# Shared scattering of two small expert groups, k maxima a slice ahead, and another order of the attention front

## The chip, the cores and the metric

The kernel runs on one core of a Trainium2 chip. A core has the matrix engine (TensorE, "PE" in the profile), the vector engine (VectorE, "DVE"), the scalar engine (ScalarE, "ACT"), GpSimd ("POOL") and SyncE ("SP", which here issues the loads and stores). Each engine works through its own queue of instructions in order and waits on semaphores for the others. The metric is the device time of one execution in microseconds (us).

## The reference

The computation has three stages. First comes an attention without a score matrix: the softmax of q runs over the head's 64 features, that of k over the 576 positions, and each head multiplies q by the 64x64 product of k and v. Its output is x, 2304 tokens of 512 features. Then two mixture-of-experts layers follow, each token going to the expert with the highest logit.

```
q_s = exp(q - max(q, over d));  q_s /= sum(q_s, over d) + 1e-9      # [4, 8, 576, 64]
k_s = exp(k - max(k, over s));  k_s /= sum(k_s, over s) + 1e-9
x   = einsum(q_s, einsum(k_s, v))                                   # as 2304 x 512

# layer 1: expert = argmax(x @ w_gate); at most 576 tokens of one expert are kept
out[i] = gate_w[i] * (relu(x[i] @ w1[e]) @ w2[e])      # 512 -> 1024 -> 512, 8 experts

# layer 2, with its own weights, only for tokens with x @ w_skip > 0
out[i] = x[i] + gate_w[i] * (relu(x[i] @ w1[e]) @ w2[e])
```

## The kernel before

**Data.** x is kept transposed, one tile X[b] for each batch b: 128 feature rows, 4 chunks of features, 576 tokens. A batch's 8 heads are two halves of 4 heads, named a and b (batch 0), c and d (1), e and f (2), g and i (3). A half goes through the attention in small steps, the methods of `Half`: `qm` (maxima of q, negated, in `mx`), `q1` to `q3` or `exp_sub` with `exp_act` (exp), `qn` or `inverse` with `norm` (division by the sums `qz`), `qt` or `turn` (transposes of q), `km` (column maxima of k, three operations on DVE that leave `m`), `kt` (transposes of m, tile `pt`, L386), `kc` (subtraction), `ke` (exp), `kv` (products k·v, into `kd`, shown as `kvd`), `re` (products q·kv, tile `px`, copied into x by ACT).

**Dense groups.** Nearly all tokens of a batch go to one expert, so for the five pairs of layer and batch in the table `COURSE`, (0,0), (0,1), (0,2), (1,0) and (1,1), the kernel runs that expert over all 576 tokens of the batch, with a gate (`gm`, `pg`, `mg`) that is zero elsewhere. Each of these groups has 16 slices, 8 for w1 and 8 for w2. A float32 operand is split into a high and a low part (`split`: ACT casts the high part `wh` or `xh`, DVE subtracts, giving `wl` or `xl`), and each product is three matmuls of 128 x 288 (`products`, `first_products`; lines L822, L842, L863). A slice runs in this order: `products(i)`, `split_w(i+2)`, the words of its line in `COURSE` to the left of the bar, `evacuate(i)` (ACT's relu `hh`, L876, and DVE's remainder `hl`, L877, or the gated sums), and then the words to the right of the bar. So the table sets the order of instructions on every engine. A word like `d.km` is a method of a half, `G.0` one of the gate's, `L4` a load of weights, `S.u00` a step of a small group.

**Small groups.** The few tokens of other experts, at most 32 for an expert, go through `Small`: S is the group of (0,2) with one expert, T that of (1,2) with two experts. Words `t` are the steps of an expert (`expert(t, step)`; the last one leaves its output in `y2`, a high and a low part: four quarters of partitions), `v` and `a` make the one-hot matrix pT of the tokens' places (`places`, `place`), and `u` scatters, `put`: for two chunks of features and two halves of tokens, two matmuls `pts` (L1255, 128 x 288 each, over all 128 partitions) and an addition to x on DVE (L1259). `y2` is zero outside of what an expert has written. `S.u00 S.u01` stand in the last slice of (0,2); `T.u00`, `T.u01` in slices 3 and 4 of (1,1), and `T.u10`, `T.u11` in its slices 10 and 11.

**Front.** Ahead of `COURSE` stands the attention of batch 0 (code from L950 to L1112), written out in one order for all engines: `k_v` is the product of k and v of a half (L992), `k_v_norm` divides it, `q_norm` divides q, `q_turn` and `q_last` transpose q (L463, L470), `x_main` and `x_last` multiply by kv (L495, L489). `H01` and `H23` are the two pairs of heads in a half: exps of H01 come from a subtraction (`exp_sub`) and one large exp (`exp_act`, L344), those of H23 from small exps with the sums included (`exps`, L334). `guess` (L568 to L587) finds, from kv alone, which expert batch 0 will use, and leaves its number in `gid`; SP reads gid and then issues the first loads of weights (`ws`). `warm_up(n)` (L535) issues n dummy matmuls on PE. At the front's end `first_products` (48 matmuls, L822) does slices 0 and 1 of the first group. The lines of the front around the change are:

```
        k_v(a)
        warm_up(16)
        v_ones(b)
...
        a.exp_sub(H01, ALLJ)
...
        k_v(b)
...
        a.sum_bulk(H01, ALLJ)
        RT["C0"].guess()
...
        q_norm(a, H01)
        q_norm(a, H23)
        warm_up(8)
```

Of the kernel before, what the change touches and what calls it, by code (L numbers as in the profile page):

```python
# [95 lines left out]
    N3 | S.t04  # L96
    X3 | S.u00 S.u01
    """),
    ((1, 0), """
    L4 G.3 | g.rw  # L100
    g.rx | M2.1
# [18 lines left out]
    L5 i.rx | T.t04 C3.1  # L120
    T.v1 | T.t10 T.u00
    L6 | T.u01 C3.2 G.1
    C3.3 | T.t11 C3.4 O0.3
# [3 lines left out]
    | T.t14  # L127
    | T.u10
    | T.u11 O1.0
    | O2.0  # L130
# [8 lines left out]
def kernel(  # L139
# [810 lines left out]
    with tc.tile_pool(name="fp", bufs=1) as fp:  # L950
# [57 lines left out]

        def q_norm(h, hs):
            h.inverse(hs)  # L1010
            h.norm(hs)

# [35 lines left out]
        k_v(a)  # L1048
        warm_up(16)
        v_ones(b)  # L1050
        k_exp(b)
        a.qm()
        a.exp_sub(H01, ALLJ)
        a.exps([(2, j) for j in range(NJ)])
        a.exp_act(H01, ALLJ)
        k_v(b)
        k_v_norm(a)
        b.qm()
        a.exps([(3, j) for j in range(NJ)])
        warm_up(12)  # L1060
        b.exp_sub(H01, ALLJ)
# [4 lines left out]
        a.sum_bulk(H01, ALLJ)  # L1066
        RT["C0"].guess()
# [10 lines left out]
        H["d"].load_v()  # L1078
        q_norm(a, H01)
        q_norm(a, H23)  # L1080
        warm_up(8)
        a.turn_new()
        q_turn(a, 0)
        warm_up(3)
        q_turn(a, 1)
# [4 lines left out]
        x_main(a, 0)  # L1090
        warm_up(2)
        x_main(a, 1)
        x_last(a)
        first.split_x(0)
        first.split_x(1)
        first.split_w(0)
        warm_up(2)
        b.turn_new()
        q_turn(b, 0)
        warm_up(3)  # L1100
        q_turn(b, 1)
        q_last(b)
        first.first_products(0, range(0, 2))
        first.split_w(1)
        x_main(b, 0)
        x_main(b, 1)
        x_last(b)
        first.first_products(1, range(0, 2))
        first.split_x(2)
        first.split_x(3)  # L1110
        first.first_products(0, range(2, 4))
        first.first_products(1, range(2, 4))  # L1112
# [9 lines left out]
    class Small:  # L1122
# [69 lines left out]
        def expert(self, t, step):  # L1192
# [4 lines left out]
            if step != 2:  # L1197
                for i in {0: (0, 1), 1: (2, 3), 3: (4, 5), 4: (6, 7)}[step]:
                    w = self.tw.pop(8 * t + i)
                    for g in range(4):  # L1200
                        if i < 4:
# [4 lines left out]
                        nc.tensor.matmul(  # L1206
                            out=self.ph[32 * g:32 * g + 32, :256], lhsT=lhsT, rhs=rhs, start=(i % 4 == 0), stop=(i % 4 == 3)
                        )
                    self.load(8 * t + i + 3)
# [9 lines left out]
            elif step == 4:  # L1219
                for i in range(2):  # L1220
                    sl, cs = slice(64 * i, 64 * i + 64), slice(2 * i, 2 * i + 2)
                    src = self.ph[sl, :256].rearrange("p (c d) -> p c d", c=2)
                    nc.scalar.copy(y2[0][sl, cs], src)
                    nc.vector.tensor_sub(y2[1][sl, cs], src, y2[0][sl, cs].bitcast(F32))

        def places(self, t):
            cs = hp.tile([P, TINY], F32, name="cs2", tag="cs2")
            nc.vector.tensor_scalar(out=cs, in0=iota, scalar1=self.r["tlo"][:, t:t + 1], scalar2=None, op0=ALU.add)
            self.p4 = hp.tile([P, NJ, 4, TINY], F32, name="p4", tag="ot", bufs=3)
            bb = [P, NJ, TINY]  # L1230
            for g in range(4):
                nc.vector.tensor_tensor(
                    out=self.p4[:, :, g],
                    in0=self.r["z"].unsqueeze(2).to_broadcast(bb),
                    in1=cs.unsqueeze(1).to_broadcast(bb),
                    op=ALU.is_equal,
                )
# [11 lines left out]

        def put(self, t, i):  # L1250
            for c in (2 * i, 2 * i + 1):
                for a in range(2):
                    pt = bank("pts")
                    for n, u in enumerate(y2):
                        nc.tensor.matmul(  # L1255
                            out=pt[:, :HT], lhsT=u[:, c], rhs=self.pT[t][:, tokens(a)], start=(n == 0), stop=(n == 1)
                        )
# [223 lines left out]
```

## Time and profile before

| quantity | value |
|---|---|
| three runs, median (lowest to highest) | 416.97 us (416.24 to 419.02) |
| the profiled execution | 416.55 us |
| its span, first to last instruction | 414.7 us |
| PE busy in it | 393.7 us |
| fillers L535 | 94 matmuls, 18.7 us |
| scattering L1255 | 48 matmuls |

All times of the sections below are those of the profiled execution, in us from the start of its span. Busy times of matmuls overlap in PE's pipeline, so a sum of them can exceed the span; the distance from one matmul's start to the next one's start tells what it costs. In a row of a timeline the columns are start, duration, engine, line, operation, written tile, read tiles, sizes and count, and in brackets the idle time ahead of it with the instruction that ended it.

### The profile page before, as it was taken

How to read it: one execution, taken by the hardware profiler on the slowest of the kernel's cores; microseconds unless marked ns; L12 is line 12 of the kernel's file. 1: busy time of each engine (PE TensorE's matmuls, PEld its weight loads, DVE VectorE, ACT ScalarE, POOL GpSimd, SP SyncE). 2: the span in 40 equal slices, each digit the busy share in tenths (PEclk: the TensorE clock that was granted, in tenths of full speed). 3: DMA queues.
4: the chain of work that ended last, by engine and by line, in shares of the span. 5: the costliest groups of instructions: out<-in, count | busy, mean ns of one | idle time of the engine just before them, and what ended most of it. 6: DMA issues, size and time to landing. Idle time of an engine off the chain costs nothing.

```text
span 414.7 us, 8456 instructions
## 1 busy us (share of the span) xinstructions
PE 393.7 (95%) x3241; PEld 351.1 (85%) x3241; DVE 251.6 (61%) x640; ACT 182.3 (44%) x547; POOL 12.4 (3%) x46
## 2 busy tenths in 40 slices
PE   8989898999999999999999999999999999899892
PEld 4656797898999989799999888899998988799881
DVE  4874789463586846278546656367777736654432
ACT  1656675734357772324346622333375342331211
POOL 2400000000000000000000100000000000000000
PEclk9999999999999999999999999999999999999998
DMA  8829926100970400293355771116315556363133
GB/s 207 220 54 262 255 72 193 31 2 2 295 182 9 124 2 2 82 300 96 107 195 178 217 216 52 51 52 232 101 53 183 182 180 214 92 204 123 31 101 102
DMA packets 72535, 54.48 MB, mean 131 GB/s; under 512 B 18454, under 2 KB 67114, under 8 KB 72490
## 3 DMA queue, kind: packets, MB, share of 16 engines
q1 hardware_dynamic: 70536, 53.60, 44.4%
q10 hardware_dynamic: 1954, 0.31, 0.6%
q8 instruction: 26, 0.43, 0.4%
q14 instruction: 19, 0.16, 0.1%
HBM read 49.16 MB, written 4.73 MB: 130 GB/s over the span
## 4 chain that ended last, share of the span: by engine, by line
PE 85%; DVE 8%; ACT 3%; issue 2%; DVEq 0%; ACTq 0%
PE pair L863 31%; PE pair L842 25%; PE pair L535 3%; PE px L495 3%; PE pxs L1150 2%; PE pk L437 2%; PE pl L596 2%; PE pto L1284 2%; PE ph L1206 1%; PE py L1206 1%; PE pts L1255 1%; PE pk L992 1%; PE ptq L463 1%; DVE hl L877 1%; PE pair L822 1%
## 5 line engine op out<-in xcount | busy, mean ns | idle before, releaser
L863 PE MATMUL pair<-hh,wh 128*128 128x288 f32 x320 | 98.3, 307 | 0.0
L863 PE MATMUL pair<-hh,wl 128*128 128x288 f32 x320 | 94.6, 296 | 0.0
L863 PE MATMUL pair<-hl,wh 128*128 128x288 f32 x320 | 94.5, 295 | 0.0
L842 PE MATMUL pair<-xh,wh 128*128 128x288 f32 x304 | 92.8, 305 | 0.0
L842 PE MATMUL pair<-xl,wh 128*128 128x288 f32 x304 | 89.6, 295 | 0.0
L842 PE MATMUL pair<-xh,wl 128*128 128x288 f32 x304 | 89.5, 295 | 0.0
L785 DVE TENSOR_TENSOR wl<-ws,wh 128x512 fp32r<-128x512 f32 x80 | 54.9, 686 | 35.9 <-ACT wh L784 35.4
L863 PEld LDWEIGHTS pair<-hh,wh 128*128 128x128 f32 x320 | 60.5, 189 | 3.8 <-issue 2.6
L863 PEld LDWEIGHTS pair<-hl,wh 128*128 128x128 f32 x320 | 60.7, 190 | 0.1
L876 ACT ACTIVATE hh<-pair 128x576 fp32r<-128x576 f32 x40 | 25.8, 645 | 79.2 <-PE pair L842 77.4
L863 PEld LDWEIGHTS pair<-hh,wl 128*128 128x128 f32 x320 | 60.5, 189 | 0.0
L842 PEld LDWEIGHTS pair<-xh,wh 128*128 128x128 f32 x304 | 57.1, 188 | 2.2 <-issue 0.9
L842 PEld LDWEIGHTS pair<-xl,wh 128*128 128x128 f32 x304 | 57.2, 188 | 0.1
L842 PEld LDWEIGHTS pair<-xh,wl 128*128 128x128 f32 x304 | 57.1, 188 | 0.0
L877 DVE SCALAR_TENSOR_TENSOR hl<-pair,hh 128x576 fp32r<-128x576 f32 x40 | 30.2, 755 | 37.1 <-ACT hh L876 37.1
L784 ACT CAST wh<-ws 128x512 fp32r<-128x512 f32 x80 | 49.3, 620 | 2.2 <-DMA ws<-in_moe_w_dram 1.5
L334 ACT ACTIVATE eq<-qt,mx 128x64 f32<-128x64 f32 x140 | 46.7, 338 | 0.5 <-DVE mx L323 0.5
L334 ACT ACTIVATION_READ_ACCUMULATOR eq<-qt,mx 128x1 f32 x140 | 26.6, 190 | 0.0
L535 PE MATMUL pair<-warm 128*128 128x384 f16 x94 | 18.7, 346 | 1.6 <-DVE warm L952 1.6
L785 DVE TENSOR_TENSOR xl<-x,xh 128x576 fp32r<-128x576 f32 x20 | 14.9, 752 | 6.0 <-ACT xh L784 6.0
L1285 ACT COPY ot<-pto 128x256 f32<-128x256 f32 (+1 forms) x24 | 7.0, 315 | 26.0 <-PE pto L1284 26.0
L535 PEld LDWEIGHTS <-warm 128*128 128x128 f16 x94 | 9.3, 104 | 8.1 <-issue 2.1
(210 smaller groups left out, 500.2 us busy)
## 6 DMA issues: line engine op xcount, KB each, us to landing
ws<-in_moe_w_dram SPq DMA_DIRECT2D x39, 512.0 KB, 4.7
tw<-in_moe_w_dram SPq DMA_DIRECT2D x24, 512.0 KB, 4.6
kt<-in_k_dram SPq DMA_DIRECT2D x8, 512.0 KB, 7.5
qt<-in_q_dram SPq DMA_DIRECT2D x8, 512.0 KB, 6.5
out_dram<-ot SPq DMA_DIRECT2D x12, 256.0 KB, 2.7
vt<-in_v_dram SPq DMA_DIRECT2D x16, 128.0 KB, 4.8
vt<-in_v_dram SPq DMA_DIRECT2D x3, 512.0 KB
mg<-gate SPq DMA_DIRECT2D x4, 288.0 KB, 7.2
```

Of the source, the lines that this page charges most:

```text
L334: nc.scalar.activation(self.eqv[:, h, j], self.qt[:, h, j], AF.Exp, bias=self.mx[:, i:i + 1], accum_out=self.qz[:, i:i + 1])
L437: nc.tensor.matmul(out=pk[64 * g:64 * g + 64, c * D1 + o:c * D1 + o + n], lhsT=self.kt[:rows(j), 2 * c + g, j], rhs=ones32[:rows(j), 0:1] ...
L495: nc.tensor.matmul(out=pt, lhsT=self.kd[:, c], rhs=self.qT[:, c, 0:4 * P], start=True, stop=True)
L535: nc.tensor.matmul(out=pw[:, 0, :3 * P], lhsT=warm16[:, 0:P], rhs=warm16, start=True, stop=True)
L596: nc.tensor.matmul(out=pl[32 * c:32 * c + 32, :HT], lhsT=self.weights[:, c], rhs=self.chunk(c, tokens(a)), start=True, stop=True,)
L784: nc.scalar.copy(hi, src)
L785: nc.vector.tensor_tensor(out=lo, in0=src, in1=hi.bitcast(F32), op=ALU.subtract)
L842: nc.tensor.matmul(out=self.pt[:, a, :HT], lhsT=u[:, c], rhs=w[:, c, tokens(a)], start=(c == 0 and n == 0), stop=(c == NC - 1 and n == 2),)
L863: nc.tensor.matmul(out=self.pt[:, a, :HT], lhsT=p_[:, f], rhs=w[:, tokens(a)], start=(v == 0 and f == 0 and n == 0), stop=(v == 1 and f == ...
L876: nc.scalar.activation(halves(hh), src, AF.Relu)
L877: nc.vector.scalar_tensor_tensor(out=halves(hl), in0=src, scalar=0.0, in1=halves(hh).bitcast(F32), op0=ALU.max, op1=ALU.subtract,)
L1150: nc.tensor.matmul(out=self.px[:, c * self.w:(c + 1) * self.w], lhsT=self.xt[:rows(j), c * P:(c + 1) * P], rhs=self.pj[:rows(j), j], start ...
```

## The change

Three things change. Names are as above.

1. **Scattering.** `put(t, i)` becomes `put(i)`. The second expert of T (t = 1) writes its outputs to the mirrored halves of the partitions of `y2`, and `places` builds one-hots of both experts into each pT, so that one set of matmuls scatters both. `T.u00` and `T.u01` are gone; `T.u10`, `T.u11` become `T.u0`, `T.u1` in the same slices. `S.u00 S.u01` become `S.u0` in the same slice and `S.u1` behind the evacuation of the first slice of (1,0).
2. **Maxima of k.** `d.km`, `e.km` and `f.km` move from the left side of a slice's bar to the right side of the bar one slice earlier.
3. **Front.** The subtraction for H01 goes from DVE to GpSimd (`q_sub`). `k_v(b)` stands behind 4 instead of 16 fillers, the sums and the first `q_norm` of a stand ahead of `guess`. The turns and products of b stand between those of a and ahead of all dense products, which now follow one another. Fillers are 74 instead of 94.

The diff, with one of the three moved maxima and the code of the front and of the scattering (the lines of dots are places left out):

```
-    C0.5 c.qn d.q1 |
-    L7 d.km | c.qt d.kt
+    C0.5 c.qn d.q1 | d.km
+    L7 | c.qt d.kt
...
-    X3 | S.u00 S.u01
+    X3 | S.u0
     """),
     ((1, 0), """
-    L4 G.3 | g.rw
+    L4 G.3 | S.u1 g.rw
     g.rx | M2.1
...
-    T.v1 | T.t10 T.u00
-    L6 | T.u01 C3.2 G.1
+    T.v1 | T.t10
+    L6 | C3.2 G.1
...
-    | T.u10
-    | T.u11 O1.0
+    | T.u0
+    | T.u1 O1.0
...
-        def q_norm(h, hs):
+        def q_norm(h, hs, eng=None):
             h.inverse(hs)
-            h.norm(hs)
+            (eng or nc.vector).tensor_tensor(
+                out=h.eqv[:, hs], in0=h.eqv[:, hs], in1=h.spread_q(h.qz, hs, ALLJ), op=ALU.mult
+            )
+
+        def q_sub(h):
+            nc.gpsimd.tensor_tensor(
+                out=h.eqv[:, H01], in0=h.qt[:, H01], in1=h.spread_q(h.mx, H01, ALLJ), op=ALU.add
+            )
 
         def q_turn(h, c):
             pt = bank("ptq")
...
         warm_up(2)
         k_sub(b)
         k_v(a)
-        warm_up(16)
         v_ones(b)
         k_exp(b)
         a.qm()
-        a.exp_sub(H01, ALLJ)
+        q_sub(a)
+        warm_up(4)
+        k_v(b)
         a.exps([(2, j) for j in range(NJ)])
         a.exp_act(H01, ALLJ)
-        k_v(b)
         k_v_norm(a)
         b.qm()
+        q_sub(b)
         a.exps([(3, j) for j in range(NJ)])
-        warm_up(12)
-        b.exp_sub(H01, ALLJ)
+        a.sum_bulk(H01, ALLJ)
+        warm_up(6)
         k_v_norm(b)
         b.exps([(2, j) for j in range(NJ)])
         b.exp_act(H01, ALLJ)
         b.exps([(3, j) for j in range(NJ)])
-        a.sum_bulk(H01, ALLJ)
+        q_norm(a, H01)
         RT["C0"].guess()
         first.eid = load_reg(gid[0], [ET.SP], 7)
         first.load(0, 0)
...
         H["d"].load_q()
         H["d"].load_k()
         H["d"].load_v()
-        q_norm(a, H01)
-        q_norm(a, H23)
-        warm_up(8)
+        warm_up(2)
         a.turn_new()
         q_turn(a, 0)
-        warm_up(3)
+        q_norm(a, H23)
+        warm_up(4)
         q_turn(a, 1)
         q_last(a)
         b.sum_bulk(H01, ALLJ)
...
         q_norm(b, H23)
         x_main(a, 0)
         warm_up(2)
+        b.turn_new()
+        q_turn(b, 0)
         x_main(a, 1)
         x_last(a)
-        first.split_x(0)
-        first.split_x(1)
-        first.split_w(0)
         warm_up(2)
-        b.turn_new()
-        q_turn(b, 0)
-        warm_up(3)
         q_turn(b, 1)
         q_last(b)
-        first.first_products(0, range(0, 2))
-        first.split_w(1)
+        first.split_x(0)
         x_main(b, 0)
+        first.split_x(1)
+        warm_up(2)
         x_main(b, 1)
         x_last(b)
-        first.first_products(1, range(0, 2))
+        first.split_w(0)
+        warm_up(4)
+        first.first_products(0, range(0, 2))
         first.split_x(2)
         first.split_x(3)
+        first.split_w(1)
+        first.first_products(1, range(0, 2))
         first.first_products(0, range(2, 4))
         first.first_products(1, range(2, 4))
...
                     w = self.tw.pop(8 * t + i)
                     for g in range(4):
+
+                        o = 32 * (g ^ 2 if t and i >= 4 else g)
                         if i < 4:
                             lhsT, rhs = self.xs[:, i, 32 * t:32 * t + 32], w[:, 256 * g:256 * g + 256]
                         else:
                             lhsT = self.hT[:, g % 2, 32 * (i - 4):32 * (i - 4) + 32]
                             rhs = w.rearrange("p (u d) -> p u d", u=2)[:, g % 2, 256 * (g // 2):256 * (g // 2) + 256]
                         nc.tensor.matmul(
-                            out=self.ph[32 * g:32 * g + 32, :256], lhsT=lhsT, rhs=rhs, start=(i % 4 == 0), stop=(i % 4 == 3)
+                            out=self.ph[o:o + 32, :256], lhsT=lhsT, rhs=rhs, start=(i % 4 == 0), stop=(i % 4 == 3)
                         )
                     self.load(8 * t + i + 3)
             if step == 1:
...
                 nc.vector.tensor_copy(out=self.hT, in_=pt[:, :2 * P].rearrange("p (u s) -> p u s", u=2))
             elif step == 4:
                 for i in range(2):
-                    sl, cs = slice(64 * i, 64 * i + 64), slice(2 * i, 2 * i + 2)
+                    o = 64 * (i ^ t)
+                    sl, cs = slice(o, o + 64), slice(2 * i, 2 * i + 2)
                     src = self.ph[sl, :256].rearrange("p (c d) -> p c d", c=2)
                     nc.scalar.copy(y2[0][sl, cs], src)
                     nc.vector.tensor_sub(y2[1][sl, cs], src, y2[0][sl, cs].bitcast(F32))
 
         def places(self, t):
-            cs = hp.tile([P, TINY], F32, name="cs2", tag="cs2")
-            nc.vector.tensor_scalar(out=cs, in0=iota, scalar1=self.r["tlo"][:, t:t + 1], scalar2=None, op0=ALU.add)
+            cs = hp.tile([P, 2, TINY], F32, name="cs2", tag="cs2")
+            for u in range(self.n):
+                nc.vector.tensor_scalar(
+                    out=cs[:, u], in0=iota, scalar1=self.r["tlo"][:, u:u + 1], scalar2=None, op0=ALU.add
+                )
             self.p4 = hp.tile([P, NJ, 4, TINY], F32, name="p4", tag="ot", bufs=3)
             bb = [P, NJ, TINY]
             for g in range(4):
                 nc.vector.tensor_tensor(
                     out=self.p4[:, :, g],
                     in0=self.r["z"].unsqueeze(2).to_broadcast(bb),
-                    in1=cs.unsqueeze(1).to_broadcast(bb),
+                    in1=cs[:, (g // 2) ^ t if self.n == 2 else 0].unsqueeze(1).to_broadcast(bb),
                     op=ALU.is_equal,
                 )
 
...
             nc.tensor.transpose(pt[:, 0:LAST], p4f[:LAST, 4], ident[:LAST, :LAST])
             nc.scalar.copy(pT[:, 4 * P:S], pt[:, 0:LAST])
 
-        def put(self, t, i):
+        def put(self, i):
+            pT = self.pT[i if self.n == 2 else 0]
             for c in (2 * i, 2 * i + 1):
                 for a in range(2):
                     pt = bank("pts")
                     for n, u in enumerate(y2):
                         nc.tensor.matmul(
-                            out=pt[:, :HT], lhsT=u[:, c], rhs=self.pT[t][:, tokens(a)], start=(n == 0), stop=(n == 1)
+                            out=pt[:, :HT], lhsT=u[:, c], rhs=pT[:, tokens(a)], start=(n == 0), stop=(n == 1)
                         )
                     x = self.x[:, c, tokens(a)]
                     nc.vector.tensor_add(x, x, pt[:, :HT])
```

The order of instructions at three places where it moves. First GpSimd's queue in the front, as a difference of the two programs; `va` and `vt` hold v of half b, `eq` and `qt` the exps and q of a (and then b), `mx` the negated maxima.

```order
 L985 COPY va<-vt 128x4x64 x4
 L985 COPY va<-vt 64x4x64
+L1016 ISA
+L1016 TENSOR_TENSOR eq<-qt,mx 128x2x5x64 x2
 L297 MEMSET kt 64x4x64
 L302 MEMSET vt 128x20
```

Two subtractions have come in behind the copies of v and ahead of the fills for later halves, with one instruction of another kind ahead of them.

Next DVE's queue in the front, from the subtraction of b to the guess, as a difference; L1003 to L1007 are `k_v_norm`, L320 and L323 `qm`, L348 the sums, L362 to L367 (L1011 in the change) `q_norm`, L572 the start of the guess.

```order
-L339 TENSOR_TENSOR eq<-qt,mx 128x2x5x64
+L348 TENSOR_REDUCE qz<-eq 128x10
 L1003 TENSOR_SCALAR rz<-pk 128x2
 L1004 RECIPROCAL rz<-rz 128x2
 L1007 TENSOR_TENSOR kvd_115<-pk,rz 64x2x64 x2
-L348 TENSOR_REDUCE qz<-eq 128x10
+L362 TENSOR_SCALAR qz<-qz 128x10
+L363 RECIPROCAL qz<-qz 128x10
+L1011 TENSOR_TENSOR eq<-eq,qz 128x2x5x64
 L572 COPY gx<-pgx 128x4
```

The subtraction is gone (that of a is gone ahead of it in the same way), the sums of a have moved ahead of the norm of kv(b), and the first norm of a's q stands ahead of the guess instead of behind it.

Last DVE's queue in the second half of the first dense group, where the maxima of d are made (L378 to L380, tile m) between the remainders `hl` of two slices; of before:

```order
L877 SCALAR_TENSOR_TENSOR hl<-pair_83,hh 128x576
L785 TENSOR_TENSOR wl_206<-ws_198,wh_202 128x512
L378 TENSOR_TENSOR m_959<-kt 128x512
L379 TENSOR_TENSOR m_960<-m_959 128x256
L380 TENSOR_TENSOR m_960<-m_960,kt 128x256
L877 SCALAR_TENSOR_TENSOR hl<-pair_84,hh 128x576
```

and of the change:

```order
L877 SCALAR_TENSOR_TENSOR hl<-pair_84,hh 128x576
L378 TENSOR_TENSOR m_912<-kt 128x512
L379 TENSOR_TENSOR m_913<-m_912 128x256
L380 TENSOR_TENSOR m_913<-m_913,kt 128x256
L785 TENSOR_TENSOR wl_206<-ws_198,wh_202 128x512
L877 SCALAR_TENSOR_TENSOR hl<-pair_83,hh 128x576
```

The three operations for m now stand ahead of the split `wl`, which stands behind them.

## Rows read from the trace of the kernel before

**Rows 1.** Page, part 1: busy us, share of the span, instructions of each engine.

```profile
PE 393.7 (95%) x3241; PEld 351.1 (85%) x3241; DVE 251.6 (61%) x640; ACT 182.3 (44%) x547; POOL 12.4 (3%) x46
```

**Rows 2.** PE's waits: line, waited for; us in total, times, longest.

```profile
PE pt L386 <- DVE m L380: 3.4, 4, 1.6
```

**Rows 3.** PE's timeline of the front: start, us, engine, line, operation, count.

```profile
16.75 2.77 PE L535 MATMUL pair<-warm 128*128 128x384 f16 x16
19.36 2.98 PE L992 MATMUL pk<-va,kt 128*128 128x130 f32 x20
...
29.28 0.63 PE L463 MATMUL ptq<-c,eq 128*128 128x128 f32 x4
...
36.01 0.40 PE L822 MATMUL pair<-xh,wl 128*128 128x288 f32 x1 [0.44 <-DVE wl L785]
...
37.44 1.88 PE L495 MATMUL px<-qT,kvd 128*128 128x512 f32 x4
...
39.52 0.38 PE L822 MATMUL pair<-xh,wh 128*128 128x288 f32 x1
...
45.17 1.18 PE L596 MATMUL pl<-x,wg 128*32 128x288 f32 x16
```

**Rows 4.** DVE's timeline of the front.

```profile
17.02 0.83 DVE L339 TENSOR_TENSOR eq<-qt,mx 128x640 f32<-128x640 f32 x1
...
22.38 0.16 DVE L1003 TENSOR_SCALAR rz<-pk 128x2 f32<-128x2 f32 x1 [1.05 <-PE pk L992]
...
23.40 0.82 DVE L348 TENSOR_REDUCE qz<-eq 128x10 f32<-128x640 f32 x1
25.22 0.16 DVE L572 COPY gx<-pgx 128x4 f32<-128x4 f32 x1 [1.01 <-PE pgx L568]
...
26.62 0.14 DVE L587 TENSOR_SCALAR gid<-gid 1x1 int32<-1x1 int32 x1
...
27.86 0.17 DVE L362 TENSOR_SCALAR qz<-qz 128x10 f32<-128x10 f32 x1
...
29.05 0.81 DVE L348 TENSOR_REDUCE qz<-eq 128x10 f32<-128x640 f32 x1
```

**Rows 5.** Timelines of POOL and of ACT in the front.

```profile
15.19 1.76 POOL L985 COPY va<-vt 128x256 f32<-128x256 f32 x5 [2.29 <-DMA vt<-in_v_dram]
...
1.80 1.28 ACT L221 ACT_TABLE_LOAD   x1 [1.80 <-issue]
...
18.69 0.72 ACT L344 ACTIVATE eq<-eq 128x640 f32<-128x640 f32 x1
```

**Rows 6.** Page, part 6: DMA issues, count, KB each, median us to landing.

```profile
ws<-in_moe_w_dram SPq DMA_DIRECT2D x39, 512.0 KB, 4.7
...
kt<-in_k_dram SPq DMA_DIRECT2D x8, 512.0 KB, 7.5
```

**Rows 7.** Timelines of DVE and PE around the maxima of d.

```profile
68.72 0.68 DVE L785 TENSOR_TENSOR wl<-ws,wh 128x512 fp32r<-128x512 f32 x1
...
71.13 0.41 PE L386 MATMUL pt<-c,m 128*128 128x128 f32 x2 [1.64 <-DVE m L380]
...
80.37 1.52 PE L936 MATMUL pg<-c,gm 128*128 128x128 f32 x10
```

**Rows 8.** Windows, line L1255 alone: S.u00 with S.u01, T.u00, T.u01; length, PE.

```profile
253.38:256.63 3.25, 2.83 (x16) 2.21 (x16) 1.00 0.58 166
347.92:349.38 1.46, 1.44 (x8) 1.13 (x8) 1.00 0.56 101
352.55:354.97 2.42, 1.32 (x8) 1.02 (x8) 1.00 0.57 165
```

**Rows 9.** Windows: length, PE, PEld, DVE, ACT, POOL, granted clock, DMA, GB/s.

```profile
1.55:4.55 3.00, 3.00 (x10) 1.48 (x11) 0.00 (x0) 1.49 (x2) 1.83 (x9) 1.00 0.80 215
4.55:7.23 2.68, 2.68 (x19) 1.58 (x17) 1.54 (x3) 0.00 (x0) 0.00 (x0) 1.00 1.19 273
410.70:414.70 4.00, 0.00 (x0) 0.00 (x0) 0.00 (x0) 0.00 (x0) 0.00 (x0) 0.50 0.17 45
```

More of the change, by code (lines that the diff above doesn't have):

```diff
@@ L1007, in k_v_norm, with q_norm, q_sub @@
                 nc.vector.tensor_mul(h.kd[sl, :, sl], pv[sl, :, g, 0:D], rz[sl].to_broadcast([64, 2, D]))
-        def q_norm(h, hs):
+        def q_norm(h, hs, eng=None):
             h.inverse(hs)
-            h.norm(hs)
+            (eng or nc.vector).tensor_tensor(
+                out=h.eqv[:, hs], in0=h.eqv[:, hs], in1=h.spread_q(h.qz, hs, ALLJ), op=ALU.mult
+            )
+        def q_sub(h):
+            nc.gpsimd.tensor_tensor(
+                out=h.eqv[:, H01], in0=h.qt[:, H01], in1=h.spread_q(h.mx, H01, ALLJ), op=ALU.add
+            )
         def q_turn(h, c):
@@ L1048 @@
         k_v(a)
-        warm_up(16)
         v_ones(b)
@@ L1052 @@
         a.qm()
-        a.exp_sub(H01, ALLJ)
+        q_sub(a)
+        warm_up(4)
+        k_v(b)
         a.exps([(2, j) for j in range(NJ)])
         a.exp_act(H01, ALLJ)
-        k_v(b)
         k_v_norm(a)
         b.qm()
+        q_sub(b)
         a.exps([(3, j) for j in range(NJ)])
-        warm_up(12)
-        b.exp_sub(H01, ALLJ)
+        a.sum_bulk(H01, ALLJ)
+        warm_up(6)
         k_v_norm(b)
@@ L1078 @@
         H["d"].load_v()
-        q_norm(a, H01)
-        q_norm(a, H23)
-        warm_up(8)
+        warm_up(2)
         a.turn_new()
         q_turn(a, 0)
-        warm_up(3)
+        q_norm(a, H23)
+        warm_up(4)
         q_turn(a, 1)
@@ L1091 @@
         warm_up(2)
+        b.turn_new()
+        q_turn(b, 0)
         x_main(a, 1)
         x_last(a)
-        first.split_x(0)
-        first.split_x(1)
-        first.split_w(0)
         warm_up(2)
-        b.turn_new()
-        q_turn(b, 0)
-        warm_up(3)
         q_turn(b, 1)
         q_last(b)
-        first.first_products(0, range(0, 2))
-        first.split_w(1)
+        first.split_x(0)
         x_main(b, 0)
+        first.split_x(1)
+        warm_up(2)
         x_main(b, 1)
         x_last(b)
-        first.first_products(1, range(0, 2))
+        first.split_w(0)
+        warm_up(4)
+        first.first_products(0, range(0, 2))
         first.split_x(2)
         first.split_x(3)
+        first.split_w(1)
+        first.first_products(1, range(0, 2))
         first.first_products(0, range(2, 4))
@@ L1200, in expert @@
                     for g in range(4):
+                        o = 32 * (g ^ 2 if t and i >= 4 else g)
                         if i < 4:
@@ L1206, in expert @@
                         nc.tensor.matmul(
-                            out=self.ph[32 * g:32 * g + 32, :256], lhsT=lhsT, rhs=rhs, start=(i % 4 == 0), stop=(i % 4 == 3)
+                            out=self.ph[o:o + 32, :256], lhsT=lhsT, rhs=rhs, start=(i % 4 == 0), stop=(i % 4 == 3)
                         )
@@ L1226, in places @@
         def places(self, t):
-            cs = hp.tile([P, TINY], F32, name="cs2", tag="cs2")
-            nc.vector.tensor_scalar(out=cs, in0=iota, scalar1=self.r["tlo"][:, t:t + 1], scalar2=None, op0=ALU.add)
+            cs = hp.tile([P, 2, TINY], F32, name="cs2", tag="cs2")
+            for u in range(self.n):
+                nc.vector.tensor_scalar(
+                    out=cs[:, u], in0=iota, scalar1=self.r["tlo"][:, u:u + 1], scalar2=None, op0=ALU.add
+                )
             self.p4 = hp.tile([P, NJ, 4, TINY], F32, name="p4", tag="ot", bufs=3)
@@ L1255, in put @@
                         nc.tensor.matmul(
-                            out=pt[:, :HT], lhsT=u[:, c], rhs=self.pT[t][:, tokens(a)], start=(n == 0), stop=(n == 1)
+                            out=pt[:, :HT], lhsT=u[:, c], rhs=pT[:, tokens(a)], start=(n == 0), stop=(n == 1)
                         )
```

34 lines of the change are left out of this document (18 added, 16 removed).

## The prediction

> **What bounds the kernel now.** I read four views. First, busy time by engine: TensorE (PE) works 393.7 of 414.7 us, DVE 251.6, ACT 182.3, POOL 12.4 [rows 1]. Time is won where PE has less to do or stands less. Second, what PE waited for [rows 2]: its largest entry is four waits, together 3.4 us, of the transposes `pt` for the column maxima `m` of k, which DVE makes. That view hides the front, because fillers (the dummy products of `warm_up`, L535) count as busy. So the third view is PE's timeline of the front, read for what the fillers cover [rows 3]. k_v(a) is done when sixteen fillers start at 16.75; k_v(b) starts only behind them, at 19.36. The second turn of half a starts at 29.28, the long run of dense products (`first_products`, L822) at 36.01, and it ends at 45.17, where the router's logits start; between 37.44 and 39.52 the x of half b cuts it. Fourth, DVE's timeline tells who sets this pace [rows 4]. At 22.38 it has waited 1.05 us for k_v(b); then come the norm of kv(b), a's sums (23.40) and the guess (its copy at 25.22, gid ready at 26.62 + 0.14 = 26.76). Only behind the guess stand the two norms of a's q, the second from 27.86 to 29.05, and the turn at 29.28 needs the second. So the front's chain is k_v(b), DVE's norm, sums, guess and norms, the turns and x of both halves, dense products. Behind 45.17 PE is nearly dense, so what the front saves reaches the end unless a later wait takes it up.
>
> **The front.** Four edits act on this chain.
>
> (1) k_v(b) stands behind 4 fillers instead of 16. Sixteen take 19.36 − 16.75 = 2.61, 0.163 each [rows 3]; k_v(b) starts at 16.75 + 4 × 0.163 = 17.40, 1.96 earlier, and so ends at about 20.4 instead of 22.38.
>
> (2) DVE no longer makes the differences q − max of a and b (0.83 each, the first at 17.02) [rows 4]; POOL does. From 17.02 to 22.38 − 1.05 = 21.33 DVE made both of these, the norm of kv(a) and b's maxima; without the two that is 4.31 − 1.66 = 2.65, so until 19.7. Then a's sums, 0.82, to 20.5; the norm of kv(b), 23.40 − 22.38 = 1.0, to 21.5; a's first q norm, taken like the second's 29.05 − 27.86 = 1.2, to 22.7; from the guess's copy to gid 26.76 − 25.22 = 1.54, to 24.2 (2.5 earlier; the first loads of `ws` wait for gid, and come earlier by as much); the second q norm to 25.4. The second turn of a starts then, 3.8 ahead of 29.28.
>
> (3) From there PE runs the turns and x of a and b's turns as before, 36.01 − 29.28 = 6.73, and now x of b too, 39.52 − 37.44 = 2.08: dense products start at 25.4 + 6.7 + 2.1 = 34.2. Fewer fillers could shorten it, but b's norms follow a's on DVE at the same distance, so I keep the 6.73.
>
> (4) All 48 dense products then run in one piece. Without a wait one takes (37.44 − 36.01) / 10 = 0.143, so 48 take 6.9; with the waits of before, (45.17 − 36.01 − 2.08) / 46 = 0.154, so 7.4. With 7.2 they end at 41.4 against 45.17: **−3.7**; ends −4.0 and −3.5. What could be late is their operands, the splits of x and w by ACT and DVE; one more wait as at 36.01 (0.44) is about the upper end.
>
> The price of the move is POOL's. In before POOL only copies and fills: five copies of 256 elements take 1.76, 0.35 each, until 16.95 [rows 5]. By that, 640 elements are 0.9 if only their count matters; twice that, 1.8, if two inputs are read in turn. Starting at 17.0 this is ready at 17.9 or 18.8. ACT is busy with other exps until it takes this half at 18.69 [rows 5]: hidden in both cases, with 0.8 of cover left or none. The fills queued behind it on POOL are for tiles read only in the dense groups. But the order shows one more instruction there, L1016 ISA, which the built program calls a library reload; before has none. It costs nothing if there is nothing to load. The nearest row is ACT's load of a table, 1.28 [rows 5]; if code has to be fetched by a transfer, the transfers here need 4.7 to 7.5 from issue to landing [rows 6]. I take 1.28, because it is a load that an engine does for itself, like this one; the transfer is rival B. Of 1.28, the cover of 0 to 0.8 hides a part, and 0.3 more is hidden since DVE takes a's sums at 19.7 and ACT's exp (0.72) would be done at 19.4: 0.2 to 1.0 late, **+0.7**, ends 0 and +1.3. Beyond its cover every us on POOL is a us on the chain, for a's sums, the norm of kv(b), the guess and the second norm stand behind it on DVE in that order.
>
> The Trainium skill speaks against this edit: "GPSIMD Engine Reference", §2.1 Instruction dispatch, says that the first call to a freshly loaded kernel pays a code load of about 6 us with no instruction in the profile. No row of before shows such a load. By it this term would be an estimated +5.3 and the sum −1.8.
>
> **The maxima of k.** For d, e and f, DVE makes them ahead of one split `wl` (0.68 at 68.72) instead of behind it [rows 7], so each of three waits can shrink by up to 0.7; d's is 1.64 [rows 7], the others share 3.4 − 1.64, 0.6 each [rows 2]. The split itself comes later by m's three operations, but its products are a slice away. Does PE keep the gain? For d I think not: the gate's ten matmuls start at 80.37 [rows 7], behind ACT's copies of c's x, and ACT's place there follows from work on DVE and ACT that isn't less. For e there is a like join in `gate1`, behind DVE's gm. Only f's is kept: **−0.6**; ends −1.9 and 0.
>
> **The shared scattering.** For T, 16 of 32 matmuls L1255 go, and 8 adds on DVE. The two pieces removed from the middle of group (1,1) took 1.46 and 2.42 [rows 8]; less about 0.2 of pipeline change at their borders: **−3.7**, ends −3.9 and −3.4. The matmuls that stay are as wide as before, and those in the tail are as many as before; half as many do because each partition half now holds one expert's part. One more small operation of `places` on DVE lies beside PE's products. For S no matmul goes; sixteen in one piece took 3.25 [rows 8]. Now its second half stands behind the first evacuation of the next group, as T's second piece did: 1.46 + 2.42 = 3.88, up to 0.3 more for waits on the adds, so **+0.9**, ends +0.6 and +1.2.
>
> **Sum.** −3.7 + 0.7 − 0.6 − 3.7 + 0.9 = −6.4. The profiled execution took 416.55 (span 414.7 and 1.85 around it); the median of the three runs, 416.97, is 0.42 above it. From halfway between, 416.8, I take **410.4**. All low ends together are 2.8 less, all high ends 2.0 more; they don't fall together, so the sum's own range is 408.8 to 412.4. A measurement of this kernel can tell about 1%, 4.2 us, from no change.
>
> **Rivals.** A is the sum above: chance 0.66.
>
> B: the reload is a transfer of code and holds POOL for 6.1 us, the middle of 4.7 and 7.5 [rows 6]. Less 0.3 and the cover of 0 to 0.8, the exp is about 5.4 late instead of 0.7: −6.4 + 4.7 = −1.7, **415.1**. PE then stands in the front, with four fillers where it had sixteen. When PE stood still at the end of before, the granted clock was 0.50 [rows 9]; in a slow spell as at the start, where ten fillers fill 3.00 us and nineteen the next 2.68 [rows 9], 1.5 us are lost, which gives 416.6. For it: the extra instruction in the order. Against: no row of POOL's shows one. Chance 0.18. By the skill's rule this is what happens; no trace so far bears it out.
>
> C, on the other side: POOL is held longer still, by two transfers in turn. Without a reload the sum is −7.1; each us of hold behind 0.7 of cover costs one, and the slow spell 1.5, so break-even is a hold of 7.1 + 0.7 − 1.5 = 6.3 us. Two transfers, 4.7 + 7.5 = 12.2, give 416.8 + 5.9 = **422.7**. Against: POOL has one reload, ahead of the first operation. Chance 0.07.
>
> D: the front's gain is given back in the first dense groups. Loads of `ws` begin 2.5 earlier, but the maxima of c or the splits of w may be what PE meets next, as after d and e. Then of −3.7 only 2.5 stays, or nothing: 411.6 to **414.1**. For: the waits for maxima lie in the first two groups. Against: the weights come earlier too. Chance 0.09.
>
> So: faster by over 1% (under 412.8) A and a quarter of D, 0.68; within 1% B, the rest of D and a little of C, 0.27; slower 0.05. The range 408.8 to 416.8 takes in A but for its low end, B and D, and leaves out C.
>
> **What would show it.** PE's timeline: k_v(b) at 17.4, dense products from 34 and the router's logits near 42; at 46, it is B. POOL: its first tensor operation within 1.3 us of 17.0, under 1.8 long, and ACT's exp of a at 18.7 to 19.7. No long gap, and a granted clock of 1.0, in the front. PE's waits: `pt` for `m` 1.9 less in sum, with the gate of 80.37 still as far behind the front's end. Matmuls L1255: 32 instead of 48, with a wait among them at the start of (1,0). Wrong would be an exp after 22, a clock of 0.5 in the front, or new waits for `wl` or `m` behind 42.

## The result and the profile after

The changed kernel took 409.80 us in the median of three runs (409.31 to 412.97), against 416.97 before: a ratio of 0.9842 with a 95% interval of 0.9807 to 0.9877, so 1.6% faster. Its profiled execution took 409.8 with a span of 408.0; before it was 414.7, so 6.7 less. A second measurement of the same kernel later (`changed_again`) gave 0.9849 (0.982 to 0.9878); over both, nine executions lie between 409.23 and 412.97 with a median of 410.51.

The page's busy times, after, in the form of [rows 1]:

```profile
PE 388.0 (95%) x3205; PEld 347.1 (85%) x3205; DVE 247.0 (61%) x632; ACT 182.3 (45%) x547; POOL 14.7 (4%) x48
```

PE lost 36 matmuls: 20 fillers and 16 of the scattering. POOL gained the two subtractions. Next, PE's waits after, as in [rows 2] (waited for; us in total, times, longest):

```profile
PE pts L1270 <- DVE x L1274: 2.7, 3, 1.2
PE pt L386 <- DVE m L380: 1.6, 2, 1.0
...
PE pgu L575 <- DVE gx L572: 1.2, 3, 0.7
...
PE ptq L463 <- ACT qT L1023: 0.8, 1, 0.8
...
PE pg L936 <- ACT x L502: 0.5, 1, 0.5
PE pgm L918 <- DVE gm L913: 0.5, 1, 0.5
```

The waits for m fell from 3.4 in four to 1.6 in two. What is new stands below: 0.8 for the copy of a's first turn, 0.5 of the gate's products `pg` for ACT's copies of x, the join that the prediction named for d, and 0.5 of `pgm` for DVE's gm, the one that it named for e.

PE's timeline of the front, after; the rows answer to [rows 3]:

```profile
7.84 0.38 PE L386 MATMUL pt<-c,m 128*128 128x128 f32 x2
...
14.39 2.98 PE L992 MATMUL pk<-x,x 128*128 128x130 f32 x20
17.30 0.82 PE L535 MATMUL pair<-warm 128*128 128x384 f16 x4
17.96 2.98 PE L992 MATMUL pk<-va,kt 128*128 128x130 f32 x20
...
26.18 0.63 PE L463 MATMUL ptq<-c,eq 128*128 128x128 f32 x4 [0.79 <-ACT qT L1023]
...
34.60 0.40 PE L822 MATMUL pair<-xh,wh 128*128 128x288 f32 x1 [0.15 <-ACT wh L784]
...
42.00 1.18 PE L596 MATMUL pl<-x,wg 128*32 128x288 f32 x16
```

The first two rows are new and need their partners of before, the first product that needs k and k_v(a):

```profile
7.23 0.38 PE L386 MATMUL pt<-c,m 128*128 128x128 f32 x2
...
13.84 2.98 PE L992 MATMUL pk<-x,x 128*128 128x130 f32 x20
```

In this execution the first product that needs k started 0.61 later than in the one of before. In the twelve other profiles of this study it starts between 7.28 and 8.63, with all of the code up to it the same in every kernel, so the lateness belongs to the execution and not to the change. It is not the load of k that is late. The rows are DVE's last step of the maxima of k, on which that product waits, and PE's weight loads for the 26 fillers ahead of it; first of before, then of after:

```profile
6.65 0.42 DVE L380 TENSOR_TENSOR m<-m,kt 128x256 f32<-128x256 f32 x1
4.41 2.59 PEld L535 LDWEIGHTS <-warm 128*128 128x128 f16 x16 [0.17 <-issue]
...
6.79 0.42 DVE L380 TENSOR_TENSOR m<-m,kt 128x256 f32<-128x256 f32 x1
5.69 1.93 PEld L535 LDWEIGHTS <-warm 128*128 128x128 f16 x12 [0.17 <-issue]
```

The maxima were ready at 7.07 and 7.21, only 0.14 apart. The fillers run 0.32 apart until 4.41 before and until 5.69 after, and 0.16 apart from then on, so after the change PE was still busy with them when the maxima were ready. Over all fourteen profiles the maxima are ready between 7.07 and 7.46, and the product starts later where the slow stretch of the fillers lasts longer: until 4.41 in the kernel before, until 7.29 in the two profiles with 8.63. The windows give a granted clock of 1.00 on both sides of this point, as [rows 9] do, so they do not show what ends the slow stretch.

All of the front shifts with this start. The front's end came 45.17 − 42.00 = 3.17 earlier, and 3.78 earlier counted from the first product that needs k; "from k" means this below. Counted from the start of k_v(a) it lies at 31.33 before and at 27.61 after, 3.72 earlier.

From there to the end, both kernels run the same 1920 dense products in the same order, so the difference of their starts shows where time went. These are the starts of the first product of a slice, from the two timelines of PE:

| the first dense product behind | before | after | difference |
|---|---|---|---|
| the front (router's logits) | 45.17 | 42.00 | −3.17 |
| d's maxima, slice 7 of (0,0) | 71.30 | 67.52 | −3.78 |
| the gate of (0,0), slice 9 | 81.82 | 78.62 | −3.20 |
| e's maxima, slice 2 of (0,1) | 121.22 | 117.44 | −3.78 |
| the gate of (0,1), slice 4 | 128.15 | 124.97 | −3.18 |
| f's maxima, slice 7 of (0,1) | 141.91 | 138.14 | −3.77 |
| S.u0, slice 0 of (1,0) | 256.63 | 251.36 | −5.27 |
| S.u1, slice 1 of (1,0) | 259.95 | 257.15 | −2.80 |
| (no T.u00 any more), slice 4 of (1,1) | 349.38 | 345.13 | −4.25 |
| (no T.u01 any more), slice 5 of (1,1) | 355.73 | 348.99 | −6.74 |

So the terms are: front −3.17 (−3.78 from k), maxima −0.60, S +0.97, T −3.94, in sum −6.74, and the span shows 6.7. The join of d is this row of after:

```profile
77.17 1.52 PE L936 MATMUL pg<-c,gm 128*128 128x128 f32 x10 [0.50 <-ACT x L502]
```

It starts 35.17 behind the front's end; before, it was 35.20 (80.37 − 45.17, [rows 7] and [rows 3]).

The reload that the prediction priced did not show. POOL, ACT and DVE in the front, after (POOL's rows answer to [rows 5]):

```profile
15.80 1.76 POOL L985 COPY va<-vt 128x256 f32<-128x256 f32 x5 [2.88 <-DMA vt<-in_v_dram]
17.67 1.26 POOL L1016 TENSOR_TENSOR eq<-qt,mx 128x640 f32<-128x640 f32 x1
20.28 1.26 POOL L1016 TENSOR_TENSOR eq<-qt,mx 128x640 f32<-128x640 f32 x1 [1.35 <-DVE mx L323]
...
19.30 0.72 ACT L344 ACTIVATE eq<-eq 128x640 f32<-128x640 f32 x1
...
17.15 0.44 DVE L323 TENSOR_SCALAR mx<-mx 128x20 f32<-128x20 f32 x1
```

POOL's copies end at 17.56, the maxima at 17.59, and the first tensor operation starts at 17.67: there is 0.08 us between its operand and its start, and the first takes as long as the second. In the nine other profiles with this operation it starts at most 0.09 behind the later of the two. It ends at 18.93, 0.37 before ACT takes it at 19.30 with no idle time.

### The profile page after: what moved, and what is told of

The parts are those of the page before. It is cut to its first block, busy times and chain, and to the rows that moved or that the text cites. A ratio compares the mean times of both kernels' runs of the same rounds, so it can differ in the third digit from the quotient of the medians.

```text
span 408.0 us, 8377 instructions
## 1 busy us (share of the span) xinstructions
PE 388.0 (95%) x3205; PEld 347.1 (85%) x3205; DVE 247.0 (61%) x632; ACT 182.3 (45%) x547; POOL 14.7 (4%) x48
## 4 chain that ended last, share of the span: by engine, by line
PE 74%; ACT 3%; DVE 2%; issue 1%; ACTq 0%; DVEq 0%
PE pair L863 31%; PE pair L842 23%; PE pxs L1158 2%; PE pk L437 2%; PE pl L596 2%; PE pto L1299 2%; PE ph L1216 1%; PE py L1216 1%; ACT eq L334 1%; PE ptq L463 1%; PE px L495 1%; PE ptx L1173 1%; PE pts L1270 1%; PE ptl L608 1%; ACT hh L876 1%
## 5 line engine op out<-in xcount | busy, mean ns | idle before, releaser
L535 PE MATMUL pair<-warm 128*128 128x384 f16 x74 | 16.3, 363 | 1.6 <-DVE warm L952 1.6
L535 PEld LDWEIGHTS <-warm 128*128 128x128 f16 x74 | 7.6, 109 | 7.6 <-issue 3.3
```

The costliest lines, as they stand in the source:

```text
L535: nc.tensor.matmul(out=pw[:, 0, :3 * P], lhsT=warm16[:, 0:P], rhs=warm16, start=True, stop=True)
```

## The experiments

Twelve experiments ran, one of them with the changed kernel itself again. The kernel before ran beside them, with medians of 416.96, 416.96, 417.08 and 417.12. The ratios are to these.

**The parts alone.** Each is the kernel before with one of the three parts of the change.

> The kernel before with the new front only. Theory (the terms add): against the kernel before the front is worth 3.7 us, the profiled span 414.7 becomes about 411.0 and the time about 413.2; the dense products of the first group end near 42, and the distance to before stays 3.7 until the end. Rival (the front's gain lives on the moved maxima, which in the changed kernel stand in the first groups): part of it is given back at the three waits for d, e and f, and 1 to 2 us less arrive, a time near 414.5 to 415.

414.43 (six executions, 412.6 to 415.49), ratio 0.9923 (0.9891 to 0.9955). The logits start at 42.75 with the first product that needs k 1.30 later than before, so 3.72 earlier from k (and 3.71 from k_v(a)): the theory's front. Then this profile loses 1.35 us at one place. Windows (length; PE, PEld, DVE, ACT, POOL busy; granted clock; DMA; GB/s) and the row at which it starts:

```profile
66.00:68.00 2.00, 1.08 (x9) 0.84 (x8) 1.97 (x4) 1.69 (x5) 0.14 (x1) 1.00 1.08 272
68.00:70.00 2.00, 1.28 (x6) 1.31 (x7) 1.70 (x5) 0.27 (x1) 0.00 (x0) 0.65 0.55 125
70.00:72.00 2.00, 2.00 (x10) 2.00 (x9) 1.86 (x9) 0.95 (x6) 0.00 (x0) 0.50 0.80 178
72.00:74.00 2.00, 2.00 (x17) 1.97 (x15) 0.32 (x2) 1.77 (x11) 0.00 (x0) 1.00 0.04 8
...
68.72 0.66 PE L386 MATMUL pt<-c,m 128*128 128x128 f32 x2 [1.63 <-DVE m L380]
```

PE stood 1.63 us for d's maxima, and the granted clock went to 0.50; twelve products ran 0.24 apart instead of 0.13. The kernel before has a wait as long there (1.64, [rows 7]) and kept its clock in the profiled execution. So the rival's size (1 to 2 us less) appeared in part of the executions, though not by its mechanism: nothing was given back at e or f. Three executions with a mean clock of 0.995 or 0.996 took 412.60 to 413.49, around the theory's 413.2; the three at 0.991, this one among them, 415.36 to 415.49.

> The kernel before with the three moved maxima only. Theory: each of the three waits shrinks by 0.6 to 0.7 us; what d and e win is taken back a slice or two later by the gate's products, so that 0.7 us stays, a span near 414.0 and a time near 416.3, which is within what a measurement can tell. Rival (the joins took the gain back only because the front had come earlier): 1.9 us stays, a span near 412.8.

416.23 (ten executions), ratio 0.9986 (0.9976 to 0.9996). Against before the dense products are +0.52 behind the front (the first product that needs k started 0.60 later), −0.09 behind d, +0.49 behind the gate, −0.09 behind e, +0.51 behind the second gate, −0.08 behind f: 0.60 kept, 0.1 less than the theory, and 0.73 in the medians. The joins take d's and e's gains back without the new front too.

> The kernel before with the shared scattering only. Theory: T's two pieces gone from group (1,1) give 3.9 us, S's second piece moved to the next group costs 1.0, together 2.9 earlier: span near 411.8, time near 414.1. Rival (work that waits on T's later steps fills the gap): only part of the 3.9 stays, 1 to 2 us earlier in all, time near 415 to 416.

413.91 (four executions), ratio 0.9934 (0.9916 to 0.9953), span 411.8. Against before the dense products stand at +0.27 behind the front, −1.23 behind S.u0, +1.25 behind S.u1, −0.22 and −2.71 where T.u00 and T.u01 stood: S costs 1.25 − 0.27 = 0.98, T gives 1.25 + 2.71 = 3.96, the theory.

**Undoing one thing in the changed kernel.**

> The changed kernel with both pieces of S's scattering in the last slice of (0,2) again. Theory: two pieces cost 1.0 us more than one, because the second one stands behind an evacuation; in one piece the 1.0 comes back, span 407.0 against 408.0, time near 408.8. Rival (the second piece's time was spent on waits that move with it, and the first slice of (1,0) then waits longer for its operands): no change, 409.8, or a little slower.

```
-    X3 | S.u0
+    X3 | S.u0 S.u1
-    L4 G.3 | S.u1 g.rw
+    L4 G.3 | g.rw
```

409.20 (408.25 to 410.13), ratio 0.9824; its profiled span is 406.4, with the first product that needs k 0.56 earlier than in the changed kernel's profile, so 1.04 better. (In the medians it is 0.6 to 1.3, by the 409.80 and the 410.51 above.) Why two pieces cost more: the timelines of PE and DVE in the changed kernel,

```profile
249.62 0.95 PE L1270 MATMUL pts<-pT,y 128*128 128x288 f32 x6
251.00 0.53 PE L1270 MATMUL pts<-pT,y 128*128 128x288 f32 x2 [0.42 <-DVE x L1274]
...
254.54 0.95 PE L1270 MATMUL pts<-pT,y 128*128 128x288 f32 x6
256.60 0.53 PE L1270 MATMUL pts<-pT,y 128*128 128x288 f32 x2 [1.11 <-DVE x L1274]
...
255.42 0.76 DVE L877 SCALAR_TENSOR_TENSOR hl<-pair,hh 128x576 fp32r<-128x576 f32 x1 [2.33 <-ACT hh L876]
256.10 1.54 DVE L1274 TENSOR_TENSOR x<-x,pts 128x288 f32<-128x288 f32 x4
```

and of the kernel with one piece:

```profile
249.10 0.95 PE L1270 MATMUL pts<-pT,y 128*128 128x288 f32 x6
250.47 2.04 PE L1270 MATMUL pts<-pT,y 128*128 128x288 f32 x10 [0.42 <-DVE x L1274]
```

Behind the evacuation DVE has the remainder `hl` to make before the first add, and the fourth pair of matmuls waits 1.11 for a bank that this add frees; in one piece only the wait of 0.42 occurs. The theory holds.

> The changed kernel with the subtraction of q's maxima on the vector engine again (two operations of 0.83 us), all else as changed. Theory (the vector engine paces the new front): a's sums, the norm of kv(b), the first norm of q and the guess all move back by the 1.6 us of both, gid from 24.8 to about 26.4, and the end by 1.4 to 1.6 us, time near 411.3. Rival (the scalar engine's exps pace it, whose copy of the first turn releases the second turn): the scalar engine gets its operand earlier, nothing or up to 0.5 us is lost, time near 410.

```
-        q_sub(a)
+        a.exp_sub(H01, ALLJ)
-        q_sub(b)
+        b.exp_sub(H01, ALLJ)
```

411.71 (411.29 to 412.24), ratio 0.9876 (0.9854 to 0.9897): 1.2 to 1.9 us more than the changed kernel, by the 410.51 and the 409.80 above. The guess's second product starts at 24.92 against 23.52, with the first product that needs k 0.41 earlier, so 1.8 later: the vector engine paces the front. In the profile PE stood 1.13 and 0.90 us before it, and the granted clock was 0.60 and 0.55 in the four us that follow; the front's end is 2.45 later from k, so beyond the 1.8 another 0.6 was lost there.

> The changed kernel with GpSimd's subtraction for half a done twice (the same values, 1.26 us more on GpSimd). It measures the cover of that operation. Theory: in the changed kernel it ends at 18.93 and the scalar engine wants it at 19.30, so 0.37 of the 1.26 is covered and 0.9 us goes one for one to the scalar engine's exp, the sums, the guess and the second turn: time 0.8 to 0.9 later, near 410.6. Rival (there is more cover behind it on the vector engine): no change, 409.8.

```
+        q_sub(a)
         q_sub(a)
```

412.18 (410.72 to 413.87), ratio 0.9885 (0.9845 to 0.9924). ACT's exp now waits for POOL, and it is the first wait of this kind:

```profile
19.99 0.74 ACT L344 ACTIVATE eq<-eq 128x640 f32<-128x640 f32 x1 [0.91 <-POOL eq L1016]
```

0.91 of the 1.26 is not covered, as the theory had it; a's sums, the guess and the second turn (26.82 against 26.18) are about 1.0 later from k, and 0.9 from k_v(a). But the front's end is 3.6 later from k. The rest is lost in a stretch in which the granted clock fell. Windows of this kernel:

```profile
23.00:25.00 2.00, 1.10 (x16) 0.89 (x16) 1.43 (x6) 2.00 (x11) 0.00 (x0) 1.00 0.02 4
25.00:27.00 2.00, 1.67 (x9) 0.77 (x8) 1.86 (x7) 1.79 (x9) 0.00 (x0) 0.60 0.00 0
27.00:29.00 2.00, 2.00 (x7) 1.29 (x7) 1.86 (x6) 0.75 (x2) 0.00 (x0) 0.50 0.78 231
29.00:31.00 2.00, 2.00 (x6) 0.78 (x5) 0.88 (x2) 0.59 (x1) 0.00 (x0) 0.50 0.72 164
31.00:33.00 2.00, 2.00 (x9) 1.35 (x7) 0.00 (x0) 0.60 (x2) 0.00 (x0) 0.69 1.06 335
```

So the term was right for the chain and too small for the time: what the cover does not hide of POOL's work costs one for one here, and in a part of the executions a fall of the clock comes on top. The one execution of the four with a mean clock of 0.996 took 410.72; the others, at 0.988 to 0.989, 411.67 to 413.87.

> The changed kernel with 16 fillers instead of 4 ahead of k_v(b). Theory (the fillers, not a wait, held k_v(b) back): k_v(b) starts 12 x 0.163 = 1.96 us later, norm of kv(b), guess and the second turn move by nearly as much, and the end by 1.8 to 2.0 us, time near 411.7. Rival (the scalar engine's exps are ready no earlier anyway): at most 0.5 us later, 410.3.

```
         q_sub(a)
-        warm_up(4)
+        warm_up(16)
```

411.26 (411.01 to 411.86), ratio 0.9863. The logits start at 44.31, 1.86 later from k: the theory's 1.8 to 2.0. k_v(b) itself starts 1.95 later behind k_v(a) (20.27 − 14.75 against 17.96 − 14.39), and the front's end as well. In the medians it is 0.75 to 1.46. The fillers had held k_v(b) back.

**Keeping what the joins took.**

> The changed kernel with the gate's products of group (0,0) one slice step later (behind the slice's products instead of behind c's x) and the gate's values of (0,1) a step earlier on the vector engine. Theory (d's and e's gains of 0.58 and 0.60 us were taken back by these two joins): both stay, 1.2 us earlier, time near 408.6. Rival (the joins only show a lateness that sits in the scalar or vector engine's queue, and it appears at the next wait): nothing or little stays, 409.4 to 409.8.

```
-    d.ke | c.re G.0
-    d.q3 X0 | d.kv
+    d.ke | c.re
+    d.q3 X0 G.0 | d.kv
...
-    L5 C1.6 e.q2 | G.3 e.kc
+    L5 C1.6 e.q2 G.3 | e.kc
```

413.40 (ten executions, 411.04 to 417.03), ratio 0.9912: slower than the changed kernel, against both. The edit itself made a wait: G.0's values now stood on DVE behind the split of x, which waits for ACT.

```profile
82.06 1.49 PE L936 MATMUL pg<-c,gm 128*128 128x128 f32 x10 [2.33 <-DVE gm L913]
...
82.00:84.00 2.00, 1.94 (x20) 1.79 (x22) 0.04 (x1) 0.78 (x3) 0.00 (x0) 0.88 0.00 0
84.00:86.00 2.00, 2.00 (x32) 1.65 (x28) 0.71 (x1) 1.53 (x3) 0.00 (x0) 0.50 0.00 0
86.00:88.00 2.00, 2.00 (x12) 1.87 (x11) 1.34 (x5) 0.00 (x0) 0.45 (x2) 0.50 0.04 8
88.00:90.00 2.00, 2.00 (x10) 2.00 (x10) 1.93 (x4) 0.00 (x0) 0.00 (x0) 0.50 0.00 0
```

PE stood 2.33 us, and half a clock followed for some 6 us. At the second gate 0.6 was won. The next kernel mends the first edit by `d.q3 G.0 X0 | d.kv`; it ran beside the changed kernel itself.

> The changed kernel itself, beside the two that follow. Both theories: 409.5 to 410 in the median; runs in which k arrives late or in which the granted clock falls once lie above.

410.72 (six executions, 409.23 to 412.89), ratio 0.9849 (0.982 to 0.9878), in the median 0.7 above the upper end of what was expected. In this profile the first product that needs k started at 8.63 (the maxima were ready at 7.34, but the slow stretch of the fillers lasted until 7.29), and the clock fell at the guess:

```profile
24.28 0.35 PE L575 MATMUL pgu<-wg,gx 128*1 128x8 f32 x8 [0.71 <-DVE gx L572]
...
23.00:25.00 2.00, 1.29 (x16) 0.99 (x16) 1.46 (x5) 2.00 (x11) 0.56 (x3) 0.86 0.00 0
25.00:27.00 2.00, 2.00 (x10) 1.34 (x9) 1.83 (x8) 1.69 (x9) 0.00 (x0) 0.50 0.00 0
27.00:29.00 2.00, 2.00 (x10) 1.43 (x9) 1.86 (x6) 0.75 (x2) 0.00 (x0) 0.79 0.71 197
```

The first profile of the same kernel has the same wait of 0.71 and 1.00 in these windows. The fall cost 0.6 (logits at 43.37, 1.37 later, with the first product that needs k 0.79 later).

> The changed kernel with the gate's products of (0,0) behind the products of slice 9, and this time with its values made ahead of the split of x, so that they are not late themselves; the gate's values of (0,1) as in gate_later. Theory (the joins take d's and e's gains back): both stay, 1.0 to 1.2 us earlier than the changed kernel, near 408.6, and no wait for gm over 0.3. Rival (the lateness sits in the scalar engine's queue and shows at the next wait): no more than 0.5 us earlier, e's share alone, near 409.3.

409.04 (407.64 to 411.09), ratio 0.9805 (0.9776 to 0.9834): 1.5 to 1.7 less than the changed kernel's medians of 410.72 and 410.51, and 0.8 less than its first, 409.80. Against the changed kernel's first profile the dense products stand at +1.35 behind the front (a late start and a clock fall in the front, as in changed_again), +0.44 behind the gate of (0,0), −0.15 behind that of (0,1): 0.9 and 0.6, and no wait for gm is among PE's larger ones. Both gains stay, as the theory had it. The 0.9 is 0.3 more than the join of d had taken back; where these 0.3 come from stays open.

> The changed kernel with S's scattering in one piece and the gates as in gate_ahead_of_split. Theory (the two gains lie in different groups and add): 2.0 to 2.2 us earlier than the changed kernel, near 407.6. Rival: only the one piece of S counts, 1.0 earlier, near 408.7.

407.61 (407.08 to 408.66), ratio 0.9773 (0.9749 to 0.9797). Products at +0.31 behind the front, −0.59 and −1.16 behind the gates, −2.00 behind S: the two gains add, 2.3 us.

> The kernel both_mended with 4 fillers between the two products of the first guess and 8 instead of 4 ahead of a's second turn, where TensorE stands 0.7 and 0.8 us in the front. Theory (these waits make the granted clock fall in some executions): the two waits shrink to under 0.3 us, the clock stays at 1.00 there, no execution shows a mean clock under 0.992 that the profile puts in the front, and the median is that of both_mended, 407.6, or up to 0.3 less; 8 fillers of 0.163 lie within the waits and cost nothing. Rival (the clock falls for a reason that the fillers don't touch): the falls stay in a part of the executions, or the fillers push the second turn back and 0.3 to 0.6 us are lost, near 408.

```
         q_norm(a, H23)
-        warm_up(4)
+        warm_up(8)
...
             gx = self.tl([P, NC], "gx")   # in guess, behind the first product
+            if g == 0: warm_up(4)         # stands ahead of this line
```

407.45 (five executions, 406.89 to 408.04), ratio 0.9767 (0.9742 to 0.9791), the fastest here, but not apart from both_mended. The two waits shrank, and the clock of the front was 1.00. Counted from k_v(a) the front's end lies at 27.62, in both_mended at 27.61, so the added fillers cost nothing:

```profile
22.59 0.81 PE L535 MATMUL pair<-warm 128*128 128x384 f16 x4
...
23.00:25.00 2.00, 1.95 (x21) 1.24 (x20) 1.36 (x9) 2.00 (x10) 0.00 (x0) 1.00 0.00 0
25.00:27.00 2.00, 1.86 (x13) 1.07 (x11) 1.90 (x5) 0.98 (x4) 0.00 (x0) 1.00 0.12 33
```

No execution's mean clock is under 0.994. But of both_mended's five only one is (0.992), and its own profile, with waits of 0.72 and 0.79 at these places, also shows 1.00 there. So five executions don't settle whether fillers keep the clock up; it fits the theory and stays open.

## Why the prediction was right, point by point

Forecast 410.4, measured 409.8 (and 410.5 over nine executions); forecast of the sum −6.4, measured −6.7 in the span, −7.3 counted from k.

- **The front, −3.7:** −3.78 from k in the changed kernel, −3.72 alone. Counted from k_v(a) it is 3.71 to 3.74 in all of them: the front's end lies at 31.33 or 31.35 in the three profiles with the old front, and at 27.61 or 27.62 in the five with the new front as it stands and no fall of the clock in it. The working held step by step, each shifted by the 0.61: k_v(b) at 17.96 (17.40 + 0.61 = 18.01), the second turn at 26.18 (25.4 + 0.6 = 26.0), dense products from 34.60 (34.2 + 0.6 = 34.8), 48 of them in 7.40 (7.2); the dense products start 0.2 early and take 0.2 longer, which cancels. fillers_back and sub_on_vector show that (1) and (2) carry it. From k_v(a), 3.65 of the 3.72 are there at a's second turn, and (3) and (4), the new order behind it, add 0.07; they were not undone on their own. What was left out: ACT's copy of the first turn is released as late (26.07) as DVE's second norm (26.03), so the second turn has two engines behind it; had DVE been quicker still, ACT would have been next.
- **The subtraction on POOL:** 1.26 us, between the bounds of 0.9 and 1.8; hidden with 0.37 to spare. sub_twice shows that beyond this every us counts.
- **The reload, +0.7: this term was wrong.** It measured 0, the lower end. The operation starts 0.08 behind its operand. Rivals B and C fall with it. The rule of the Trainium skill that spoke for B ("GPSIMD Engine Reference", §2.1 Instruction dispatch) is not borne out by any trace here: none of the ten profiles with this operation shows a code load. Whether one is paid once, ahead of these executions, no run shows. That the total came out near the forecast is in part luck: the front started 0.61 later in the profiled execution of the changed kernel, which hides most of the 0.7; without both, the sum −7.1 stands beside −7.3.
- **The maxima, −0.6:** −0.60 in the changed kernel and in maxima_alone. The two joins named for d and e took back 0.58 and 0.60; moving the joins (gate_ahead_of_split) brought them in.
- **S, +0.9:** +0.97; **T, −3.7:** −3.94, the 0.2 taken off for the borders was not lost.
- **D (the front's gain given back)** did not come: the difference stays between −3.17 and −3.78 until S.
- **The slow spell, part of B,** came without B: in sub_twice, sub_on_vector, gate_ahead_of_split and in one of two profiles of the changed kernel the clock fell in the front. It was priced at 1.5; it cost 0.6 in changed_again and about 2.6 in sub_twice. The prediction named a clock of 0.5 in the front as a sign of being wrong; in these executions it came although the chain held.

## What to carry to other kernels

In kernels whose bound engine is nearly full, follow dense work that both versions share and read the difference of its starts: each edit is then one step in a table, and what a later join takes back shows at its place. Count from a start that stands behind what varies between executions, here k_v(a), and ask what the engine itself was doing before a late start is put down to a load. A gain ahead of a join on another engine was worth nothing here until the join moved too; look for the next wait behind the one that shrinks, and let what it waits for stand ahead of anything slow in its own queue. A helper engine off the path is free only up to its cover, which one run with its work doubled measures.

## What the runs showed that was not expected

The granted clock of TensorE fell in the middle of the work, from 1.00 to 0.50, after waits as short as 0.71 us (changed_again, at the guess) and 1.63 us (front_alone, at d's maxima), and came back after some 3 to 7 us. The same program with the same waits kept 1.00 in other executions, the first profile of the changed kernel among them. The kernel before stood 1.64 at d's maxima and kept 1.00 in its profile. What decides stays open.

The start of the front is uncertain by as much as a term of the sum: the first product that needs k starts between 7.23 and 8.63 over all fourteen profiles, while the maxima that it waits for are ready between 7.07 and 7.46. The product starts 0.16 behind the maxima in the kernel before and 1.46 behind them in gate_ahead_of_split, the difference being fillers that PE still had to run. So by an estimate from these rows the 26 fillers hold this product back by up to 1.3 us. A kernel with fewer of them was not run, and how much of it would reach the end is not shown.
